# Pooled attention and a rational MoE on one core: the pooled keys of batches 2 to 7 turned by VectorE and placed by transfers, and the planner's figures changed

## The chip, the cores and the metric

The kernel runs on one core of a Trainium2 chip, as one launch. The metric is the device time in microseconds (us). PE is TensorE (PEld its weight loads), DVE is VectorE, ACT is ScalarE, POOL is GpSimd, SP is SyncE, whose queue issues every transfer of this kernel.

## The reference, cut to what matters

There are 8 batches of 576 tokens, 8 heads, 64 dimensions a head. Keys and values are averaged over groups of 8 tokens, so each head has 72 pooled keys. The attention output, 4608 rows of 512, goes through two matrix products with a rational function between them.

```python
k_p = k.reshape(B, H, Sp, pool, D).mean(axis=3)      # pool 8, Sp 72
v_p = v.reshape(B, H, Sp, pool, D).mean(axis=3)
scores = scale * np.matmul(q, k_p.transpose(0, 1, 3, 2))
scores = scores - np.max(scores, axis=-1, keepdims=True)
attn = np.exp(scores)
attn = attn / (np.sum(attn, axis=-1, keepdims=True) + 1e-09)
x = np.matmul(attn, v_p)        # then laid out as 4608 x 512
h = x @ w_in                    # 512 x 2048
P = a[0] + a[1] * h + a[2] * h2 + a[3] * h3
Q = 1.0 + np.abs(b[0]) * np.abs(h) + np.abs(b[1]) * h2
out = (P / (Q + 1e-6)) @ w_out  # 2048 x 512
```

Inputs are float32 or float64 and results float32: a value is split into a high and a low part, and a product is three matrix products of parts. The weights come as float64 and are decoded on the chip.

## The kernel before, in words

**The work.** The tokens are cut into blocks: three short ones of 256 (`SHORT`) and ten of 384, numbered 0 to 12. For each block the attention (`attend`, L833) makes x, and then eight slices of the hidden layer follow (`u` from 0 to 7): `mm1` (tile `ph`), `rational`, `mm2` (tile `po`). The order of slices (L1033 on) is: blocks 0 to 2 with the first four slices, block 3 with all eight, blocks 0 to 2 with the last four (x is reloaded), then blocks 4 to 12. The weights are loaded and decoded (`load_weights`, L515) when their first user comes, which is in the first 180 us.

**The keys.** A batch is prepared when the first block that touches it is attended: batches 0 and 1 with blocks 0 and 2, batches 2 to 7 with blocks 4, 5, 7, 8, 10 and 11. `prep_k` (L550) loads the keys of a batch as 576 rows of 8 x 64 numbers, in five pieces (for batches 2 to 7 through the three `stage` buffers, which `prep_v` uses too). Three halvings sum the 8 tokens: two in place (`st_k`), and the third into `ks`, written twice over so that each row holds its 64 sums two times. POOL does the sums of batches 1 and 2, DVE those of the others. Then PE transposes the five pieces of 128 x 128 into the PSUM tiles `pk` and `pl`, and five copies (two on ACT, three on DVE) take them to `kpT` and multiply by 1/8. `kpT[n % 2]` holds, for each pair of heads, the 64 dimensions of one head in the lower half of the partitions and those of the other in the upper half, with 2 x 72 columns; the score products (tile `ps`, in `attention`, L698) read it. There are two of these tiles, so batch n writes over batch n - 2.

**The order of the work.** A planner (`Plan`, L104 on) takes the operations as the program adds them (`add`, L151), each with an engine, a cost in us and a due time, and places them by a list schedule (`solve`, L195): what can start first goes first, the one that is due first among those. Instructions are then issued in this order, and each engine works through its own in order. A due time is `HEAD + SLOW * min(at, SLOWS) + PACE * max(0, at - SLOWS)` where `at` counts the work of the MoE before it; an operation that others need is due earlier by 1.4 times (cost + 0.25 us, and 4 us more for a transfer) for each link of the chain. No operation is planned earlier than `early` before its due time (40 us, a transfer 60 us). `LATER` shifts the due times of single operations by number. Costs are written at the calls, for example `act(CW + 200)` for the first step of a decoded weight.

**Fillers.** Where the plan leaves PE idle, `issue` (L293) puts small products that change nothing (L317), on tile `idle` near the start and on `po` later.

All other instructions carry line L325, since one line issues them; they are told apart by tile.

Of the kernel before, what the change touches and what calls it, by code (L numbers as in the profile page):

```python
# [107 lines left out]
class Plan:  # L108
# [42 lines left out]
    def add(self, eng, cost, calls, port=False, claims=(), bytes=0, early=40.0, after=()):  # L151
        op = Op()
        op.eng, op.cost, op.port, op.calls, op.bytes = eng, cost, port, calls, bytes
        op.early, op.slack, op.lead = early, self.slack, 0.0
        op.keep, op.spare = self.keep, 0
        op.seq, op.due, op.deps, op.users = len(self.ops), self.now, set(), []
        touched = {}
        for _, args, kw in calls:
            every = list(args) + list(kw.values())
            dst = kw.get("out", args[0] if args else None)  # L160
            for v in every:
                if isinstance(v, Lazy) and v is not dst:
                    box = v.box()
                    op.deps.update(o for o, x in v.tile.writes if meet(x, box))
                    v.tile.reads.append((op, box))
                    touched[id(v.tile)] = v.tile
            if isinstance(dst, Lazy):
                t, box = dst.tile, dst.box()
                op.deps.update(o for o, x in t.writes if meet(x, box))
                op.deps.update(o for o, x in t.reads if meet(x, box))  # L170
                if box == ():
                    t.writes, t.reads = [], [r for r in t.reads if r[0] is op]
                t.writes.append((op, box))
                touched[id(t)] = t
        for t in touched.values():
            if t.ring.tag == "ps":

                op.deps.update(o for o in t.users if o.eng != eng)
                t.users.append(op)
        op.deps.update(after)  # L180
        op.deps.discard(op)
        for c in claims:
            touched[id(c.tile)] = c.tile
        op.bufs = list(touched.values())
        for b in op.bufs:
            b.left += 1
        self.ops.append(op)
        return op
# [155 lines left out]
def tile_pooled_attention_then_rational_moe(  # L344
# [20 lines left out]
    P = 128  # L365
# [3 lines left out]
    REM = 2 * SP - P  # L369
    RW = G * D  # L370
    SHORT, PAIR = 3, True
# [143 lines left out]
    def load_weights(kind, u):  # L515
# [12 lines left out]
        act(CW + 200).activation(m, hw.bitcast(F32), AF.Prelu, scale=2.0 ** -111, alpha=-2.0 ** 32)  # L528
        dve(CW, port=True, rate=0.52).tensor_scalar(
            out=mi, in0=mi, scalar1=3, scalar2=None, op0=ALU.logical_shift_left)  # L530
        dve(CW, port=True).scalar_tensor_tensor(
# [8 lines left out]
        act(CW + (380 if kind == "wout" else 0)).copy(high, m)  # L540
# [9 lines left out]
    def prep_k(n):  # L550
# [6 lines left out]
        pieces = ((0, 2, P), (2, 4, P)) if n < 2 else tuple((c, c + 1, P) for c in range(4))  # L557
        for c0, c1, np in (*pieces, (4, 5, H * SP - 4 * P)):
            nc_ = c1 - c0
            if n < 2:  # L560
                place = early(n, c0 // 4)[:, (c0 % 4) * RW:(c0 % 4 + nc_) * RW]
            else:
                place = new("stage", "st", [P, RW], F32, f"st_k{n}_{c0}")
            dma(2 * np * nc_, place[:np].rearrange("p (c x) -> p c x", c=nc_),
                rows[c0 * P:c0 * P + nc_ * np].rearrange("(c p) x -> p c x", c=nc_))
            st = place[:np].rearrange("p (c x) -> p c x", c=nc_)
            w = RW // 2
            while w > D:
                (gp if n in (1, 2) else dve)(nc_ * w, port=True).tensor_tensor(
                    out=st[:, :, 0:w], in0=st[:, :, 0:w], in1=st[:, :, w:2 * w], op=ALU.add)  # L570
                w //= 2
            ks = every[:np, c0:c1]
            if np < P:
                gp(2 * D).memset(every[np:, c0:c1], 0.0)
            both = [np, nc_, 2, D]
            (gp if n in (1, 2) else dve)(nc_ * 2 * w, port=True).tensor_tensor(
                out=ks, in0=st[:, :, 0:w].unsqueeze(2).to_broadcast(both),
                in1=st[:, :, w:2 * w].unsqueeze(2).to_broadcast(both), op=ALU.add)
            turns_ = [("transpose", (pk[:, c * P:(c + 1) * P] if c < 4 else pl,
                                     every[:, c].rearrange("p a d -> p (a d)"), ident), {})  # L580
                      for c in (range(c0, c1) if n < 2 else range(5))]
            if n < 2 or c1 == 5:
                turned = pe(109 * len(turns_), turns_)
                turned.lead = 1.5 if n > 2 else 0.0
        dst, both = kpT[n % 2], 2 * SP
        for hh in range(2):
# [9 lines left out]
            for to, src in parts:  # L596
                if hh == 0:
                    act(150).activation(to, src, AF.Copy, scale=1.0 / G)
                else:
                    dve(120).tensor_scalar(out=to, in0=src, scalar1=1.0 / G, scalar2=None,  # L600
                                           op0=ALU.mult)
# [76 lines left out]
    HB = 32  # L678

    def squares(i):  # L680
# [4 lines left out]
        if i < SHORT:  # L685
            return new("cpool", "wout6" if i else "win6", shape, F32, f"q{i}")
        qs = new(*(("cpool", "wout7") if i == SHORT else ("work1", "am")), shape, F32, f"q{i}")
# [10 lines left out]
    def attention(i, m, hi, lo, qs, es):  # L698
# [7 lines left out]
        if i >= SHORT:  # L706
# [38 lines left out]
        act(H * SP + 24).activation(ef, ef, AF.Exp, scale=D ** -0.5)  # L745
# [12 lines left out]
        if i >= SHORT:  # L758
# [74 lines left out]
    def attend(i):  # L833

        for _, _, n in segs(tok0(i), size(i)):
            if n not in prepared:
                prepared.add(n)
                prep_k(n)
                (prep_v_early if n < 2 else prep_v)(n)
# [4 lines left out]
        if i < SHORT:  # L844
# [9 lines left out]
        if i >= SHORT:  # L854
# [184 lines left out]
    for i, u in order:  # L1039
        for fs in ((0, 1),) if i < SHORT and PAIR else ((0,), (1,)):  # L1040
            steps.append((at, i, u, fs))
            at += len(fs) * size(i) / 512
    HEAD, PACE, SLOW, SLOWS = 15.6, 5.8, 5.48, 20
# [16 lines left out]
    for at, i, u, fs in steps:  # L1060
# [3 lines left out]
        if (i, again) not in xs:  # L1064
            plan.slack = 1.4
            plan.now = due(at) - (0 if again else {1: 8, 2: 14, 3: 14}.get(i, 0.0))
# [59 lines left out]
```

## Time and profile before

| | |
|---|---|
| median of 3 runs | 883.38 us (882.62 to 1519.48) |
| the profiled execution | 883.58 us, of which the span from first to last instruction is 881.9 us |
| PE, PEld busy | 865.2 us (98%), 805.5 us (91%) |
| DVE, ACT, POOL busy | 769.7, 725.2, 549.9 us |
| the chain that ended last | PE 82%, ACT 7%, DVE 5%, DMA 3% |

The run of 1519.48 us stands by itself and isn't used. The profile is of one execution: busy times are times in which an engine ran an instruction. PE's are modelled from pipelined instructions and overlap, so the spacing of their starts tells more than the length of one. In a list by tile, "x5" counts instructions, and the times are of one. "[0.89 <-ACT gh]" behind an instruction is the idle time of its engine just before it, and what ended it.

### The profile page before, as it was taken

The page shows a single profiled execution, that of the slowest core. Times are in us where ns is not written, and L with a number is a line of the kernel's source. Part 1 is how long each engine was busy: PE and PEld are TensorE (multiplying, and loading weights), DVE is VectorE, ACT ScalarE, POOL GpSimd, SP SyncE. Part 2 cuts the span into 40 slices and gives each one's busy share as a digit, 9 for nine tenths or more (in the row PEclk, how much of TensorE's full clock was granted, in tenths as well). Part 3 has the DMA queues.
Part 4 walks back from the last instruction along what each step waited for, and adds up shares of the span by engine and source line. Part 5 has one row for each costly group of instructions (what it writes and reads, how often), then busy time and mean ns, then how long its engine had stood idle before and what let it go on. Part 6 is the DMA issues. An engine that isn't in the chain of part 4 may idle for free.

```text
span 881.9 us, 15828 instructions
## 1 busy us (share of the span) xinstructions
PE 865.2 (98%) x5067; PEld 805.5 (91%) x5067; DVE 769.7 (87%) x1585; ACT 725.2 (82%) x1373; POOL 549.9 (62%) x614
## 2 busy tenths in 40 slices
PE   8799999999999999999999999999999999999998
PEld 7699889998999999999999999999999999999997
DVE  6899988888998988998998987998998987997764
ACT  4798898987688788788798797788888888888886
POOL 5766779796645744666655854646755764554554
PEclk9999999999999999999999999999999999999999
DMA  9896651133344232244034142043332432020000
GB/s 301 211 383 224 176 126 38 49 121 108 82 113 106 46 80 61 33 89 131 14 77 98 32 89 36 37 84 73 96 54 50 113 55 37 37 47 8 37 1 36
DMA packets 192919, 79.17 MB, mean 90 GB/s; under 512 B 169412, under 2 KB 169412, under 8 KB 192836
## 3 DMA queue, kind: packets, MB, share of 16 engines
q1 hardware_dynamic: 192836, 78.16, 34.2%
q8 instruction: 40, 0.66, 0.3%
q14 instruction: 43, 0.35, 0.1%
HBM read 52.17 MB, written 14.16 MB: 75 GB/s over the span
## 4 chain that ended last, share of the span: by engine, by line
PE 82%; ACT 7%; DVE 5%; DMA 3%; POOL 2%; issue 1%; SPq 1%; POOLq 0%; DVEq 0%; ACTq 0%
PE ph L325 36%; PE po L325 36%; PE ps L325 4%; PE pv L325 3%; DMA q<-in_q_dram 2%; DVE t L325 2%; ACT rp L325 1%; SPq L325 1%; ACT t L325 1%; PE pvs L325 1%; ACT hi L325 1%; ACT r L325 1%; ACT w L325 1%; DVE e L325 1%; ACT gh L325 1%
## 5 line engine op out<-in xcount | busy, mean ns | idle before, releaser
L325 PE MATMUL ph<-x,win 128*128 128x384 f32 (+1 forms) x2208 | 380.1, 321 | 1.1 <-POOL win L325 0.6
L325 PEld LDWEIGHTS ph<-x,win 128*128 128x128 f32 x2208 | 356.7, 190 | 12.1 <-POOL win L325 0.8
L325 PE MATMUL po<-wout,gh 128*128 128x512 f32 x1152 | 299.8, 383 | 1.8 <-ACT gh L325 1.7
L325 POOL TENSOR_TENSOR w<-w,r 128x384 f32<-128x384 f32 (+2 forms) x186 | 196.2, 1056 | 148.4 <-ACT r L325 136.8
L325 POOL TENSOR_TENSOR gl<-t,gh 128x384 fp32r<-128x384 f32 (+2 forms) x186 | 201.3, 1083 | 127.2 <-ACT gh L325 95.2
L325 PEld LDWEIGHTS po<-wout,gh 128*128 128x128 f32 x1152 | 209.4, 189 | 25.3 <-ACT gh L325 3.5
L325 DVE SCALAR_TENSOR_TENSOR t<-t,abn,rp 128x384 f32<-128x384 f32 (+2 forms) x186 | 114.7, 618 | 58.4 <-ACT rp L325 57.2
L325 PE MATMUL po<-wout,gl 128*128 128x512 f32 x576 | 162.0, 382 | 0.7 <-POOL gl L325 0.6
L325 ACT ACTIVATE t<-ph,abn 128x384 f32<-128x384 f32 (+2 forms) x186 | 125.8, 678 | 35.8 <-DVE rp L325 13.9
L325 ACT ACTIVATE r<-w,abn 128x384 f32<-128x384 f32 (+2 forms) x186 | 133.1, 715 | 9.0 <-POOL gl L325 4.1
L325 ACT ACTIVATE rp<-w,cbias 128x384 f32<-128x384 f32 (+2 forms) x186 | 110.7, 595 | 30.6 <-POOL w L325 25.8
L325 DVE TENSOR_TENSOR t<-t,ph 128x384 f32<-128x384 f32 (+2 forms) x186 | 103.6, 559 | 19.1 <-ACT w L325 10.2
L325 PEld LDWEIGHTS po<-wout,gl 128*128 128x128 f32 x576 | 104.7, 189 | 12.4 <-POOL gl L325 2.1
L325 DVE SCALAR_TENSOR_TENSOR t<-t,abn,ph 128x384 f32<-128x384 f32 (+2 forms) x186 | 114.5, 616 | 1.2
L325 ACT ACTIVATE w<-ph 128x384 f32<-128x384 f32 (+2 forms) x186 | 92.4, 497 | 21.6 <-PE ph L325 17.4
L325 ACT CAST gh<-t 128x384 fp32r<-128x384 f32 (+2 forms) x186 | 96.0, 516 | 14.6 <-DVE t L325 9.7
L325 DVE SCALAR_TENSOR_TENSOR t<-rp,t 128x384 f32<-128x384 f32 (+2 forms) x186 | 104.0, 559 | 1.9
L325 DVE SCALAR_TENSOR_TENSOR rp<-w,rp 128x384 f32<-128x384 f32 (+2 forms) x186 | 105.0, 565 | 0.0
L325 ACT ACTIVATE rp<-rp 128x384 f32<-128x384 f32 (+2 forms) x186 | 91.1, 490 | 2.2
L325 POOL TENSOR_TENSOR e<-e,sm 128x576 f32<-128x576 f32 x36 | 42.8, 1201 | 29.2 <-DVE sm L325 20.2
L325 POOL TENSOR_TENSOR st_v<-st_v 128x256 f32<-128x256 f32 (+1 forms) x72 | 42.6, 603 | 7.9 <-DMA st_v<-in_v_dram 7.2
L325 PE MATMUL ps<-kpT,qT 128*128 128x144 f32 (+1 forms) x304 | 42.0, 293 | 0.3 <-DVE qT L325 0.3
(110 smaller groups left out, 879.5 us busy)
## 6 DMA issues: line engine op xcount, KB each, us to landing
am<-e SPq DMA_DIRECT2D x160, 72.0 KB, 2.4
rwin<-in_moe_w_in_dram SPq DMA_DIRECT2D x8, 1024.0 KB, 8.2
rwout<-in_moe_w_out_dram SPq DMA_DIRECT2D x8, 1024.0 KB, 12.2
out_dram<-ob SPq DMA_DIRECT2D x30, 256.0 KB, 2.5
st_k<-in_k_dram SPq DMA_DIRECT2D x24, 256.0 KB, 3.2
st_v<-in_v_dram SPq DMA_DIRECT2D x24, 256.0 KB, 2.7
q<-in_q_dram SPq DMA_DIRECT2D x112, 48.0 KB, 2.3
xd<-x SPq DMA_DIRECT2D x6, 512.0 KB, 12.3
```

The lines of the kernel that those rows point to most:

```text
L325: getattr(engines[op.eng], name)(*map(value, args), **{k: value(v) for k, v in kw.items()})
```

## The change

For batches 2 to 7, `prep_k_late` takes the place of `prep_k`. The keys of two heads (64 of their 72 pooled rows) are loaded into one stage buffer by two transfers, four times, and the last 8 pooled rows of all heads into half of a fifth by eight. The sums go on three halvings as before, the last one without the doubling, into `squares_` (tile `ks`). DVE transposes this tile in squares of 32 x 32, in two instructions, and 16 transfers from SBUF to SBUF place the squares in `kpT`: eight of 16 KB in runs of 128 bytes, eight of 2 KB in runs of 32 bytes. The five transposes on PE, their PSUM tiles and the five copies go for these batches. Batches 0 and 1 keep `prep_k`. The factor 1/8 moves into the scale of the exponential for all batches.

For the planner: `early` is 24 us in place of 40 for all but transfers; the costs of three steps of the weight decoding are longer; `HEAD, PACE, SLOW, SLOWS` go from 15.6, 5.8, 5.48, 20 to 16.0, 5.76, 5.55, 8; the attention of block 2 is due 20 us ahead of its first use in place of 14, that of block 3 10 in place of 14; `LATER` is another list. `TURNED` takes the place of `SHORT` in the attention with the same value 3, and `PAIR` goes, which was true.

```diff
-    def add(self, eng, cost, calls, port=False, claims=(), bytes=0, early=40.0, after=()):
+    def add(self, eng, cost, calls, port=False, claims=(), bytes=0, early=24.0, after=()):
...
-        act(CW + 200).activation(m, hw.bitcast(F32), AF.Prelu, scale=2.0 ** -111, alpha=-2.0 ** 32)
+        act(CW + (480 if kind == "wout" else 350)).activation(m, hw.bitcast(F32), AF.Prelu, scale=2.0 ** -111, alpha=-2.0 ** 32)
...
-        dve(CW, port=True).scalar_tensor_tensor(
+        dve(CW + (280 if kind == "wout" else 160), port=True).scalar_tensor_tensor(
...
-        act(CW + (380 if kind == "wout" else 0)).copy(high, m)
+        act(CW + (460 if kind == "wout" else 0)).copy(high, m)
...
+    def prep_k_late(n):
+
+        MAIN = 2 * HB
+        squares_ = new("work1", "ks", [P, NJ + 1, D], F32, f"ks{n}")
+        eng = gp if n == 2 else dve
+        for c in range(NJ + 1):
+            st = new("stage", "st", [P, RW], F32, f"st_k{n}_{c}")
+            np = P if c < NJ else P // 2
+            if c < NJ:
+                for hh in range(2):
+                    dma(128, st[hh * MAIN:(hh + 1) * MAIN, :], k[n, 2 * c + hh, 0:MAIN * G, :].rearrange(
+                        "(s t) d -> s (t d)", t=G))
+            else:
+                for h in range(H):
+                    dma(16, st[h * (SP - MAIN):(h + 1) * (SP - MAIN), :],
+                        k[n, h, MAIN * G:S, :].rearrange("(s t) d -> s (t d)", t=G))
+            w = RW // 2
+            while w >= D:
+                to = st[:np, 0:w] if w > D else squares_[:np, c, :]
+                eng(w, port=True).tensor_tensor(out=to, in0=st[:np, 0:w], in1=st[:np, w:2 * w],
+                                                op=ALU.add)
+                w //= 2
+        for r in (slice(0, P), slice(0, P // 2)):
+            cs = slice(0, NJ) if r.stop == P else slice(NJ, NJ + 1)
+            dve((cs.stop - cs.start) * D).transpose(squares_[r, cs], squares_[r, cs])
+        for hh in range(2):
+            for b in range(2):
+                to = kpT[n % 2][hh * D + b * HB:hh * D + (b + 1) * HB]
+                cols = slice(b * HB, (b + 1) * HB)
+                for g in range(2):
+                    p0, s0 = hh * MAIN + g * HB, hh * SP + g * HB
+                    dma(16, to[:, :, s0:s0 + HB], squares_[p0:p0 + HB, 0:NJ, cols], run=128,
+                        issue=0.65)
+                    s0 = hh * SP + MAIN
+                    dma(2, to[:, 2 * g:2 * g + 2, s0:s0 + SP - MAIN],
+                        squares_[g * HB:(g + 1) * HB, NJ, cols].rearrange(
+                            "p (j h s) -> p h j s", j=2, h=2)[:, hh], run=32, issue=0.65)
...
-        act(H * SP + 24).activation(ef, ef, AF.Exp, scale=D ** -0.5)
+        act(H * SP + 24).activation(ef, ef, AF.Exp, scale=D ** -0.5 / G)
...
-                prep_k(n)
-                (prep_v_early if n < 2 else prep_v)(n)
+                (prep_k if n < POOLED else prep_k_late)(n)
+                (prep_v_early if n < POOLED else prep_v)(n)
...
-    HEAD, PACE, SLOW, SLOWS = 15.6, 5.8, 5.48, 20
+    HEAD, PACE, SLOW, SLOWS = 16.0, 5.76, 5.55, 8
...
-            plan.now = due(at) - (0 if again else {1: 8, 2: 14, 3: 14}.get(i, 0.0))
+            plan.now = due(at) - (0 if again else {1: 8, 2: 20, 3: 10}.get(i, 0.0))
```

In `prep_k` the branches for batches 2 to 7 go, and its copies to `kpT` no longer scale.

## Rows read from the trace of the kernel before

**Rows 1.** Busy time of each engine in five stretches of the span (length; busy us and instructions of PE, PEld, DVE, ACT, POOL; granted TensorE clock; DMA share, GB/s).
```profile
0.00:44.00 44.00, 34.88 (x237) 31.82 (x238) 33.31 (x70) 26.07 (x48) 29.82 (x69) 0.95 0.91 256
44.00:180.00 136.00, 133.31 (x850) 123.52 (x850) 122.60 (x214) 123.80 (x203) 105.36 (x84) 0.99 0.52 162
180.00:330.00 150.00, 149.58 (x932) 138.98 (x932) 137.07 (x275) 120.19 (x224) 95.08 (x105) 1.00 0.36 95
330.00:858.00 528.00, 527.74 (x2959) 493.89 (x2958) 465.24 (x1000) 440.14 (x864) 308.65 (x345) 1.00 0.26 58
858.00:882.00 24.00, 19.68 (x97) 17.31 (x95) 11.45 (x30) 15.01 (x37) 10.95 (x15) 1.00 0.09 33
```

**Rows 2.** The chain that ended last, in order of time: two unbroken pieces of PE in the steady stretch (start, us, what, how many products).
```profile
328.39 7.80 PE ph L325 x48
...
428.01 3.24 PE po L325 x15
```

**Rows 3.** The transposes of the keys by the tile `pk` (four of a batch's five; the fifth writes `pl`), all of the run.
```profile
L325 PE MATMUL pk<-identr,ks x32: 272/273/273, 6.6 to 684.9; 128*128 128x128 f32 x32
```

**Rows 4.** Timeline of PE around the transposes of batches 4 and 6, and the first scores of batch 4 (start, length, engine, instruction, count).
```profile
411.34 0.60 PE L325 MATMUL pk<-identr,ks 128*128 128x128 f32 x4
...
411.81 1.22 PE L325 MATMUL ph<-x,win 128*128 128x384 f32 x6
412.87 0.81 PE L325 MATMUL po<-wout,gh 128*128 128x512 f32 x3
...
414.16 0.65 PE L325 MATMUL ps<-kpT,qT 128*128 128x144 f32 x4
...
618.40 0.60 PE L325 MATMUL pk<-identr,ks 128*128 128x128 f32 x4
...
619.93 0.81 PE L325 MATMUL po<-wout,gh 128*128 128x512 f32 x3
```

**Rows 5.** Groups of instructions by shape (busy us of all, mean ns of one): DVE's last halvings, its transposes of other tiles, and its copies to `kpT`.
```profile
L325 DVE TENSOR_TENSOR ks<-st_k 128x128 f32<-128x128 f32 x20 | 6.7, 347 | 0.0
...
L325 DVE STREAM_TRANSPOSE qT<-q 128x512 f32<-128x512 f32 x30 | 21.1, 703 | 2.6 <-DMA q<-in_q_dram 1.9 <-DMA st_v<-in_v_dram 0.4
...
L325 DVE STREAM_TRANSPOSE e<-e 128x128 f32<-128x128 f32 x60 | 17.3, 293 | 0.3 <-POOL e L325 0.3
...
L325 DVE TENSOR_SCALAR kpT<-pk 64x216 f32<-64x216 f32 x8 | 3.1, 385 | 0.6 <-ACT kpT L325 0.4
...
L325 DVE TENSOR_SCALAR kpT<-pl 64x64 f32<-64x64 f32 x8 | 1.8, 228 | 2.8 <-PE pl L325 2.6
...
L325 DVE TENSOR_SCALAR kpT<-pk 64x8 f32<-64x8 f32 x8 | 1.3, 163 | 0.0
```

**Rows 6.** Issues on SP's queue by tile (ns of one issue, min/median/max), and below each the time from issue to landing.
```profile
L325 SPq DMA_DIRECT2D st_k<-in_k_dram x30: 327/430/1964, 104.9 to 673.1; - x30
DMA to landing us min/median/max: 2.5/3.1/4.6
...
L325 SPq DMA_DIRECT2D am<-e x160: 586/632/1863, 99.0 to 793.2; - x160
DMA to landing us min/median/max: 2.2/2.4/4.1
```

**Rows 7.** What SP's queue waited for between 330 and 858 us: the longest (us in total, times, longest).
```profile
SPq L325 <- DVE e L325: 102.6, 7, 20.0
```

**Rows 8.** The last halvings by tile, for batches 2, 5 and 7 in turn ("first to last start" is what is read).
```profile
L325 POOL TENSOR_TENSOR ks<-st_k x5: 448/490/502, 140.4 to 157.2; 128x128 f32<-128x128 f32 x4, 64x128 f32<-64x128 f32 x1
...
L325 DVE TENSOR_TENSOR ks<-st_k x5: 275/279/284, 448.6 to 469.3; 128x128 f32<-128x128 f32 x4, 64x128 f32<-64x128 f32 x1
...
L325 DVE TENSOR_TENSOR ks<-st_k x5: 271/280/285, 660.7 to 678.4; 128x128 f32<-128x128 f32 x4, 64x128 f32<-64x128 f32 x1
```

**Rows 9.** Timeline of PE: the first scores of batches 2, 5 and 7.
```profile
211.97 1.14 PE L325 MATMUL ps<-kpT,qT 128*128 128x144 f32 x8
...
480.63 0.65 PE L325 MATMUL ps<-kpT,qT 128*128 128x144 f32 x4
...
687.79 1.28 PE L325 MATMUL ps<-kpT,qT 128*128 128x144 f32 x8
```

**Rows 10.** Timeline of PE: its waits between 44 and 180 us, and the longest run of fillers.
```profile
94.19 0.70 PE L325 MATMUL po<-wout,gh 128*128 128x512 f32 x2 [0.89 <-ACT gh L325]
...
118.16 2.51 PE L317 MATMUL po<-zero,identr 128*128 128x256 f32 x21
...
121.49 0.70 PE L325 MATMUL po<-wout,gh 128*128 128x512 f32 x2 [0.82 <-ACT gh L325]
...
170.62 0.92 PE L325 MATMUL po<-wout,gl 128*128 128x512 f32 x3 [0.65 <-POOL gl L325]
```

**Rows 11.** The fillers on `po` (L317), all of the run: ns of one, first and last start.
```profile
L317 PE MATMUL po<-zero,identr x31: 272/274/276, 82.1 to 322.4; 128*128 128x256 f32 x31
```

**Rows 12.** Groups by shape: three of the steps of the weight decoding whose planned costs change (busy us of all, mean ns of one).
```profile
L325 DVE SCALAR_TENSOR_TENSOR m_wout<-rwout,m_wout 128x1024 int32<-128x1024 int32 x8 | 12.6, 1575 | 0.0
L325 ACT CAST wout<-m_wout 128x1024 fp32r<-128x1024 f32 x8 | 11.6, 1454 | 2.7 <-DVE m_wout L325 2.7
...
L325 DVE SCALAR_TENSOR_TENSOR m_win<-rwin,m_win 128x1024 int32<-128x1024 int32 x8 | 10.8, 1354 | 0.1
```

More of the change, by code (lines that the diff above doesn't have):

```diff
@@ L369, in tile_pooled_attention_then_rational_moe @@
     REM = 2 * SP - P
+    HB = 32
     RW = G * D
-    SHORT, PAIR = 3, True
+    SHORT, TURNED, POOLED = 3, 3, 2
     NBLK = SHORT + (NT - SHORT * 256) // 384
@@ L556, in prep_k @@
         every = new("work1", "ks", [P, 5, 2, D], F32, f"ks{n}")
-        pieces = ((0, 2, P), (2, 4, P)) if n < 2 else tuple((c, c + 1, P) for c in range(4))
-        for c0, c1, np in (*pieces, (4, 5, H * SP - 4 * P)):
+        for c0, c1, np in ((0, 2, P), (2, 4, P), (4, 5, H * SP - 4 * P)):
             nc_ = c1 - c0
[L560 to L563, printed above, removed]
+            place = early(n, c0 // 4)[:, (c0 % 4) * RW:(c0 % 4 + nc_) * RW]
             dma(2 * np * nc_, place[:np].rearrange("p (c x) -> p c x", c=nc_),
@@ L568, in prep_k @@
             while w > D:
-                (gp if n in (1, 2) else dve)(nc_ * w, port=True).tensor_tensor(
+                (gp if n == 1 else dve)(nc_ * w, port=True).tensor_tensor(
                     out=st[:, :, 0:w], in0=st[:, :, 0:w], in1=st[:, :, w:2 * w], op=ALU.add)
@@ L575, in prep_k @@
             both = [np, nc_, 2, D]
-            (gp if n in (1, 2) else dve)(nc_ * 2 * w, port=True).tensor_tensor(
+            (gp if n == 1 else dve)(nc_ * 2 * w, port=True).tensor_tensor(
                 out=ks, in0=st[:, :, 0:w].unsqueeze(2).to_broadcast(both),
                 in1=st[:, :, w:2 * w].unsqueeze(2).to_broadcast(both), op=ALU.add)
[L579 to L584, printed above, removed]
+            pe(109 * nc_, [
+                ("transpose", (pk[:, (c0 + c) * P:(c0 + c + 1) * P] if c0 < 4 else pl,
+                               every[:, c0 + c].rearrange("p a d -> p (a d)"), ident), {})
+                for c in range(nc_)])
         dst, both = kpT[n % 2], 2 * SP
@@ L597, in prep_k @@
                 if hh == 0:
-                    act(150).activation(to, src, AF.Copy, scale=1.0 / G)
+                    act(150).copy(to, src)
                 else:
-                    dve(120).tensor_scalar(out=to, in0=src, scalar1=1.0 / G, scalar2=None,
-                                           op0=ALU.mult)
+                    dve(120).tensor_copy(to, src)
+    def prep_k_late(n):
[34 more added lines that the diff above has]
+                            "p (j h s) -> p h j s", j=2, h=2)[:, hh], run=32, issue=0.65)
     def v_rows(n):
@@ L676, in segs @@
         return r
-    HB = 32
     def squares(i):
         shape = [P, NJ, size(i) // HB, HB]
-        if i < SHORT:
+        if i < TURNED:
             return new("cpool", "wout6" if i else "win6", shape, F32, f"q{i}")
-        qs = new(*(("cpool", "wout7") if i == SHORT else ("work1", "am")), shape, F32, f"q{i}")
+        qs = new(*(("cpool", "wout7") if i == TURNED else ("work1", "am")), shape, F32, f"q{i}")
         for r0, r1, n in segs(tok0(i), size(i)):
@@ L705, in attention @@
               new("work1", "qT", [P, NJ * P], F32, f"qT{t}")).rearrange("p (j t) -> p j t", j=NJ)
-        if i >= SHORT:
+        if i >= TURNED:
             b0 = m * (P // HB)
@@ L757, in attention @@
                 for c in range(2)]
-        if i >= SHORT:
+        if i >= TURNED:
             for c in range(2):
@@ L843, in attend @@
         es = new("work1", "e", [P, NJ + 2, M, 2 * SP], F32, f"e{i}")
-        if i < SHORT:
+        if i < TURNED:
             if not shared:
@@ L853, in attend @@
             attention(i, m, hi, lo, qs, es)
-        if i >= SHORT:
+        if i >= TURNED:
             for a in range(4):
@@ L1039, in tile_pooled_attention_then_rational_moe @@
     for i, u in order:
-        for fs in ((0, 1),) if i < SHORT and PAIR else ((0,), (1,)):
+        for fs in ((0, 1),) if i < SHORT else ((0,), (1,)):
             steps.append((at, i, u, fs))
             at += len(fs) * size(i) / 512
-    HEAD, PACE, SLOW, SLOWS = 15.6, 5.8, 5.48, 20
+    HEAD, PACE, SLOW, SLOWS = 16.0, 5.76, 5.55, 8
     def due(at):
```

23 rows, old and new, of the table LATER are left out of this document.

## The prediction, made before the changed kernel ran

> **What bounds the kernel now.** I read the busy times by stretch first [rows 1]. From 330 to 858 us PE is busy 527.74 of 528 us, from 180 to 330 us 149.58 of 150; DVE follows with 465.24 of 528 us. Busy alone could mean slow products that wait inside, so the second view is the chain of waits [rows 2]: 48 products of 384 columns take 7.80 us, 162.5 ns each, and 15 of 512 columns 3.24 us, 216 ns each. That is 384 and 512 columns at 2.4 a ns with 2 to 3 ns over: at the granted clock of 1.00, which is the level of 2.4 GHz, the array takes a column in every cycle. In this stretch time falls only if PE has less to do, and it rises by all that PE has to wait. PE's idle time is elsewhere: 44 - 34.88 = 9.1 us before 44 us, 136 - 133.31 = 2.7 us from 44 to 180 us, and 4.3 us at the end [rows 1].
>
> One page speaks against reading it so: the Trainium skill, "Perfetto Trace Analysis", section "Identifying the Most-Contended Engine", calls busy time of matmuls a bad measure of distance to the roofline and wants that of the weight loads. By that, the 493.89 us of PEld in 528 [rows 1] would leave room on PE, taking five transposes away would save nothing, and the time would be the one before. The spacing speaks against it, and the measurement decides; it is the last rival below.
>
> **Part 1: five transposes on PE go, in six batches.** The tile `pk` takes 32 transposes in the run, four a batch for eight batches [rows 3]; six of those batches lose them, with the fifth of each. A transpose is listed at 273 ns, but they overlap, so the price is read from what comes after [rows 4]. Batch 4: the first starts at 411.34, six `ph` products follow at 411.81, `po` at 412.87. The six products take 6 x 162.5 = 0.975 us by [rows 2], so the transposes put `po` back by 1.53 - 0.975 = 0.56 us. Batch 6: 619.93 - 618.40 is again 1.53. The difference between the first two starts, 0.47, is the lower bound. Six batches give 6 x 0.56 = **3.3 us** (2.8 to 3.4). All of it lies where PE is full, so it comes off the end.
>
> **Part 2: DVE, ACT and POOL.** DVE loses three copies a batch, 385 + 228 + 163 = 776 ns [rows 5]. Its last halving writes 64 columns in place of 128: by the median of 280 ns [rows 8], at about 1 ns a column, 0.06 us less, five times. It gains two transposes: from 703 ns at 512 columns and 293 at 128 [rows 5], 1.07 ns a column, 256 columns are about 0.43 us and 64 about 0.22. Net 0.4 to 0.5 us less a batch. ACT loses two copies, POOL a memset. None of these bounds the steady stretch, so I put it at 0. The factor 1/8 in the exponential changes a constant.
>
> **Part 3: SP's queue and the transfers.** For each late batch 5 loads become 16, and 16 placements come in. By 0.43 us for a load and 0.63 for an SBUF to SBUF transfer in 128-byte runs (`am`, the nearest row) [rows 6] that is 11 x 0.43 + 16 x 0.63 = 14.8 us of SP more a batch. Between 330 and 858 us SP waits in one line alone, for DVE's `e`, 102.6 us [rows 7], so its time isn't scarce; its order is what matters. Queued behind a placement that waits for DVE's transposes are the stage loads of the values, the queries of the next block, the `am` transfers and the stores of the output; DVE and then PE wait for these.
>
> Ahead of the scores the chain becomes longer. Before, batch 4's first transpose started at 411.34 and its first scores at 414.16 [rows 4], 2.8 us for PE and the copies. Now it is DVE 0.65, sixteen issues 10.1, landing 2.4 [rows 6]: **13.2 us**. Is that room there? The last halvings start at 157.2, 469.3 and 678.4 in batches 2, 5 and 7 [rows 8], the first scores at 211.97, 480.63 and 687.79 [rows 9]: 54.8, 11.3 and 9.4 us. Left where they are, batch 5 would come 1.9 us late and batch 7 3.8, each a straight loss on PE. But the due times move: a placement's is 1.4 x (0.65 + 4.25) = 6.9 us ahead of the scores, and those that write the same 32 partitions are counted one behind the other, four deep, 27 us. So the halvings are due some 30 us earlier than the scores, against about 2 before, and `early` of 24 lets them start another 24 ahead. I take 0, with 0 and 5.7 us as ends; a gain is excluded, since no wait of PE for `kpT` stands in the trace.
>
> A rule against this part: the Trainium skill, "DMA: Bandwidth & Descriptors", section "Rules for kernel authors", says to coalesce, as transfers under 64 KB pay mostly overhead. The landing of `am`, 2.4 us for 72 KB, against 3.1 for the larger `st_k` fits that: by the rule the placements of 2 and 16 KB cost nearly what 72 KB cost, and if nothing hid them the time would be the 941 us of the rival of late keys.
>
> **Part 4: the planner's figures.** The longer costs are nearer to the trace: the plan had 0.068 + 1024 x 1.04 / 1000 = 1.13 us for the decoding step that takes 1575 ns in `wout` and 1354 in `win`, and 1.26 us for a cast of 1454 [rows 12]. That stretch, 44 to 180 us, is where PE waits for ACT and POOL (0.89, 0.82, 0.65 us) and runs 21 fillers in 2.51 us before block 3's x [rows 10]; 31 fillers at 0.12 are 3.7 us [rows 11], all but the last before 180 us. Idle and fillers there are 2.7 + 3.6 = 6.3 us, the most that better order could return. Against it: block 3's attention is due 4 us later than before, which is where those fillers stand, so the same place could lose up to 4 us. I take a gain of **1.5 us**, a quarter of 6.3, since one cause of several is mended; ends +4.0 and -6.3. What lies before 44 us (9.1 us) and the last 4.3 us I leave as they are; the due times of block 1 and 2 shift in the former in either direction.
>
> **Sum.** 883.58 (the profiled execution; the median of the runs is 883.38, 0.2 below) - 3.3 - 1.5 = 878.8, so against the median **878.6 us**.
>
> **The rivals.** A kernel of this time moves by 2% only from 17.7 us on, which is about what a measurement tells from no change.
>
> *Given back in the order of the work* (chance 0.27). The 3.3 us come off PE, but the new due times put waits into the first 330 us or between stages. For it: the old list of shifts left under 0.7 us of idle PE in 678 us [rows 1], so another order has little to win and much to lose; block 3 is due later. Against it: the decoding costs are truer. One wait more of 2 to 7 us: 882 to 888 us.
>
> *Late keys, slower than before* (0.12). The placements aren't in SBUF when PE reaches the first scores of a batch, at `ps` after `kpT`, and PE, in order, stands still. Unhidden the chain costs 13.2 - 2.8 = 10.4 us a batch, 62 us in six: 941. With only batches 5 and 7 late by 1.9 and 3.8 us it is 878.6 + 5.7 = 884.3. It turns the sign when the six waits together exceed 4.8 us, 0.8 a batch, and passes 2% at 22.5 us, 3.7 a batch. For it: the room in the trace for two of six batches. Against it: the earlier due times. I give 0.08 to 884 to 901 and 0.04 to more.
>
> *More from the front* (0.08). The order before 180 us returns most of the 6.3 us and some of the 9.1: 868 to 875 us.
>
> *PE has room after all* (0.03). The transposes were covered by the weight loads, and taking them away does nothing: 882 to 883.4 us.
>
> **How the numbers follow.** The forecast, 875 to 882, has 0.50. The range takes in the rival that gives it back, whole, and the lower part of late keys: **873 to 888 us**. Left out are the rest of late keys and half of the gain from the front, about 0.14. Faster by over 2% (under 865.7) would need all idle time but the head's minimum: 0.01. Slower by over 2% (over 901.1): 0.04. Within 2%: 0.95.
>
> **What the changed profile would show.** PE's instructions on `pk` 8 in place of 32, and PE busy from 330 to 858 us as full as before, with the span shorter. 96 transfers into `kpT`, at 0.6 us an issue. The score products wait for no transfer; if they do, the late keys are there, first in batches 5 and 7. Fillers on `po` near 120 us fewer, and the waits for ACT's `gh` near 94 and 121 us gone; if they are longer, part 4 has the wrong sign. If PE is idle for more than 2 us after 330 us, the order of the work was the weak point; if the span falls by less than 2.8 us with PE full, part 1 was.

## The result, and the profile after

The changed kernel takes 894.8 us (median of 6 runs, 892.08 to 896.72) against 884.46 beside it, where one run of six, 1519.48 us, stands by itself and is left out of the ratio: ratio 1.011, 95% interval 1.0092 to 1.0128, so **9.7 us slower**, where 4.8 less were forecast and 888 was the end of the range. Within 2%, but not by the forecast's reasons. The profiled execution took 893.83 us, its span 892.1.

Busy time by stretch, of the kernel after (columns as in [rows 1]; the fourth stretch ends at 868 here):

```profile
0.00:44.00 44.00, 37.84 (x258) 34.63 (x259) 31.51 (x68) 25.50 (x48) 28.20 (x69) 1.00 0.97 270
44.00:180.00 136.00, 133.78 (x866) 125.56 (x865) 121.89 (x214) 120.13 (x197) 95.26 (x78) 0.99 0.51 158
180.00:330.00 150.00, 148.03 (x912) 136.64 (x912) 136.08 (x269) 120.13 (x222) 98.02 (x107) 1.00 0.36 96
330.00:868.00 538.00, 532.69 (x2958) 495.32 (x2957) 472.62 (x1003) 438.80 (x861) 308.98 (x343) 1.00 0.27 59
```

PE is idle 538 - 532.69 = 5.3 us behind 330 us, against 0.26 in [rows 1], and 2.0 against 0.4 between 180 and 330. The chain that ended last, by engine, where before had PE 82% and SP's queue 1%:

```profile
PE 49%; SPq 13%; DVE 12%; ACT 9%; DMA 6%; issue 5%; POOL 4%; DVEq 0%; POOLq 0%; ACTq 0%
```

By tile, the transposes on PE that are left (against [rows 3]), the placements, and the fillers (against [rows 11]):

```profile
L324 PE MATMUL pk<-identr,ks x8: 272/273/330, 8.7 to 30.6; 128*128 128x128 f32 x8
...
L324 SPq DMA_DIRECT2D kpT<-ks x96: 585/595/1590, 143.9 to 705.3; - x96
...
L316 PE MATMUL po<-zero,identr x74: 272/274/367, 66.4 to 236.9; 128*128 128x256 f32 x74
```

The change does what it says: 8 transposes for 32, 96 placements at 0.6 us an issue. What DVE waited for between 330 and 858 us, its waits for queries (`qT`) alone (before: 1.9 + 0.4 us):

```profile
DVE qT L324 <- DMA q<-in_q_dram: 4.6, 4, 1.9
DVE qT L324 <- issue: 2.1, 1, 2.1
...
DVE qT L324 <- DMA kpT<-ks: 1.6, 1, 1.6
```

SP's queue ahead of one of these waits, and the wait (timeline of after; "x27" instructions in a row, in brackets the idle time before):

```profile
468.02 0.44 SPq L324 DMA_DIRECT2D q<-in_q_dram  x1
468.56 2.51 SPq L324 DMA_DIRECT2D kpT<-ks  x4
471.11 0.59 SPq L324 DMA_DIRECT2D q<-in_q_dram  x1
471.74 0.59 SPq L324 DMA_DIRECT2D kpT<-ks  x1
472.37 1.07 SPq L324 DMA_DIRECT2D q<-in_q_dram  x2
473.48 1.24 SPq L324 DMA_DIRECT2D kpT<-ks  x2
474.76 14.49 SPq L324 DMA_DIRECT2D q<-in_q_dram  x27
...
483.22 0.71 DVE L324 STREAM_TRANSPOSE qT<-q 128x512 f32<-128x512 f32 x1 [0.82 <-DMA q<-in_q_dram]
```

For 21 us SP issues without a pause. With the placements left out (x2, below) the same queries go in one piece and the last of them is issued 8 us earlier, though x2's products are only 2.5 us ahead there:

```profile
465.16 16.01 SPq L326 DMA_DIRECT2D q<-in_q_dram  x32
```

The placements are in good time for the scores; the pieces of queries that stand in the same row are not, and it is DVE that waits for them.

### The profile page after: what moved, and what is told of

Read it like the earlier page. It is cut to its first block, busy times and chain, and to the rows that moved or that the text cites. A ratio compares the mean times of both kernels' runs of the same rounds, so it can differ in the third digit from the quotient of the medians.

```text
span 892.1 us, 16044 instructions
## 1 busy us (share of the span) xinstructions
PE 872.4 (98%) x5085; PEld 809.9 (91%) x5085; DVE 773.9 (87%) x1579; ACT 720.0 (81%) x1361; POOL 541.8 (61%) x608
## 4 chain that ended last, share of the span: by engine, by line
PE 49%; SPq 13%; DVE 12%; ACT 9%; DMA 6%; issue 5%; POOL 4%; DVEq 0%; POOLq 0%; ACTq 0%
PE ph L324 21%; PE po L324 21%; SPq L324 13%; DVE t L324 5%; PE ps L324 3%; PE pv L324 3%; ACT rp L324 2%; DMA q<-in_q_dram 2%; POOL w L324 2%; DVE rp L324 2%; DVE e L324 1%; ACT t L324 1%; DMA rwin<-in_moe_w_in_dram 1%; DMA st_v<-in_v_dram 1%; ACT gh L324 1%
## 5 line engine op out<-in xcount | busy, mean ns | idle before, releaser
L324 PEld LDWEIGHTS ph<-x,win 128*128 128x128 f32 x2208 | 357.4, 190 | 15.3 <-issue 1.6
L324 PE MATMUL po<-wout,gl 128*128 128x512 f32 x576 | 160.2, 380 | 0.0
L324 POOL TENSOR_TENSOR e<-e,sm 128x576 f32<-128x576 f32 x36 | 41.0, 1151 | 30.2 <-DVE sm L324 19.6
L324 PE MATMUL ps<-kpT,qT 128*128 128x144 f32 (+1 forms) x304 | 44.2, 294 | 0.4 <-DVE e L324 0.3
```

What stands on the lines that cost most here:

```text
L324: getattr(engines[op.eng], name)(*map(value, args), **{k: value(v) for k, v in kw.items()})
```

## The experiments

Theory 1, the order: the plan made anew (figures, due times, list of shifts) lost it. Theory 2, the queue: the 27 more transfers of a late batch did. Each run is given as its ratio to before on the same chip, with the interval; 0.001 is 0.88 us.

### The placements, taken out of two orders

In x2 the placements are skipped where instructions are issued; in y1 the same, with `LATER` empty; a0 has `LATER` empty and the placements in. So x2 and y1 leave the pooled keys of batches 2 to 7 out of the result; a0 computes all of it.

```diff
             for name, args, kw in op.calls:
+                if name == "dma_start" and isinstance(args[0], Lazy) and args[0].tile.name.startswith("kpT"):
+                    continue
```

x2: 

> The changed kernel's order with its 96 placements left out at issue, so the scores of batches 2 to 7 are taken with keys that were never placed (the pooled keys of batches 2 to 7 are left out of the result). Theory 1 (the order): the other instructions stand as badly as before; within 1.5 us of the changed kernel, 893 to 896. Theory 2 (the queue): SP gets back 16 x 0.6 = 9.6 us a batch where it now issues without a pause; 4 to 9 us faster, 885 to 890, and PE idle after 330 us falls from 5.3 to under 2.5 us.

a0: 

> The changed kernel with its new list of shifts emptied, all else as changed: what the new list is worth. Before's list was worth 0.75% on the chip (b0 against before). If the new list fits its order as well, this is 5 to 8 us slower than the changed kernel, 1.017 to 1.021 times before; if it is worth nothing on the chip, within 1.5 us of it or faster, and half of the excess over the forecast lies in that list.

y1: 

> The changed kernel with an empty list of shifts (a0) and its 96 placements left out at issue, so the pooled keys of batches 2 to 7 are left out of the scores. a0 was 1.0028 times before. If a placement costs SP's time in any order, this falls by as much as x2 did, 6 to 8 us, to 0.994 to 0.996 times before. If the placements only hurt in the order that the new list makes, within 2 us of a0: 1.001 to 1.004.

| | with placements | without |
|---|---|---|
| the new list | 1.0110 (1.0092 to 1.0128) | x2: 1.0027 (1.0016 to 1.0038) |
| no list | a0: 1.0028 (1.0014 to 1.0042) | y1: 0.9969 (0.9958 to 0.9980) |

Both theories hold, side by side. The placements cost 0.0083 under the list and 0.0059 without, 7.3 and 5.2 us; the list costs 0.0082 with them and 0.0058 without. With neither, the late keys are 2.7 us **faster** than before. DVE's waits for queries, 330 to 858 us, in x2, then a0, then y1 (the only `qT` lines among each one's ten longest):

```profile
DVE qT L326 <- DMA q<-in_q_dram: 3.0, 3, 1.9
```
```profile
DVE qT L312 <- DMA q<-in_q_dram: 5.7, 5, 2.9
...
DVE qT L312 <- issue: 0.5, 1, 0.5
```
```profile
DVE qT L314 <- DMA q<-in_q_dram: 0.6, 1, 0.6
```

After minus x2 is 8.3 - 3.0 = 5.3 us of waiting, a0 minus y1 6.2 - 0.6 = 5.6: near the 7.3 and 5.2 us that the placements cost. Counted from 180 us on, these waits are 10.8 against 3.0 us in the first pair and 6.8 against 0.6 in the second, so the differences are 7.8 and 6.2 us. SP's queue has 2% of x2's chain and 13% of after's.

When the cost comes shows where both profiles of a pair are read product by product, since their orders are the same. a0 stays within 0.2 us of y1 from the first `ph` product up to 280 us and is 4.7 us behind at the last one. The changed kernel is 1.8 us ahead of x2 at 77 us, ahead of any placement, level at 330 us, and 5.2 us behind at 751. So batch 2's placements, from 144 us on, cost next to nothing, and the later ones cost steps of up to 2 us at single places.

The number of fillers doesn't tell the loss: a0 and y1 have 80 of them on `po`, more than the changed kernel's 74, and y1 is faster than before.

### Issue or bytes, loads, another queue

x7 cuts each placement to one partition (`args = tuple(a[0:1] for a in args)`); x4 makes 5 loads of the 16; x5 issues the placements from POOL (`eng = self.nc.gpsimd`). All three have the changed kernel's order and list. x7 leaves 31 of 32 rows of the late keys out of the result, x4 has these keys in wrong places, and x5 computes everything.

x7: 

> The changed kernel with each of the 96 placements cut to one partition of its 32, so 31 of 32 rows of the pooled keys of batches 2 to 7 are left out. The issues stay, the bytes go. If SP's issue is the cost, the time stays within 1.5 us of the changed kernel, as far as an issue still takes 0.6 us (if a small one takes 0.4, a third of the 7 us that x2 gave comes back). If the transfers themselves are the cost (engines of the DMA, ports of SBUF), it falls by 5 to 7 us, to x2's 1.003 times before.

x4: 

> The changed kernel's order, but at issue the 16 loads of a late batch's keys become five of the same bytes, each at the place of the first of its group and the others dropped; the rows of the keys then stand in another order, so the scores of batches 2 to 7 are taken with keys in wrong places. SP issues 66 transfers less in the run, at 0.43 us, 28 us. Theory 1 (the order): within 1 us of the changed kernel's 1.011 times before. Theory 2 (the queue), by what x2 gave back for 96 placements (some 7 us for 58 us of SP): about half as much, 2 to 4 us faster than the changed kernel.

x5: 

> The changed kernel whole, its 96 placements issued from POOL's queue in place of SP's, at the same place in the order. If the issue in SP's queue is the cost, SP gets back what x2 gave it and the time falls 3 to 7 us below the changed kernel, unless POOL pays as much: POOL is busy 541.8 of 892 us and issues 16 a batch. If the placed bytes or the landing are the cost, no change within 1 us. If POOL's own order is as tight as SP's, the time rises by some us a batch.

x7 came to 1.0074 (1.0053 to 1.0095), about half of the way to x2; its interval just touches the changed kernel's, so the share is rough. Its issues hardly got shorter:

```profile
L326 SPq DMA_DIRECT2D kpT<-ks x96: 552/572/722, 144.9 to 702.5; - x96
```

With 1/32 of the rows an issue takes 572 ns for 595. What SP pays for these is by the transfer, not by the byte. Yet DVE's waits for queries between 330 and 858 us fall to 3.1 + 1.0 + 0.5 = 4.6 us, from 8.3 (x2 has 3.0), so the rest of the gain comes with the bytes; how they delay a query isn't shown, since these traces don't give the queries' landings. The Trainium skill, "DMA: Bandwidth & Descriptors", section "Rules for kernel authors", says that transfers under 64 KB pay mostly overhead. As far as the issue goes, the 572 ns agree. x4 is at 1.0093 (1.0073 to 1.0113): the 66 loads more can't be told from nothing. x5 is worst, 1.0205 (1.0190 to 1.0220): POOL issues in 551 ns, and ACT waits 13.2 us for its `w` between 330 and 858 us, in place of 10.1. Most of the loss is earlier: read product by product, x5 loses 4.9 us to the changed kernel between 128 and 166 us, where POOL issues batch 2's placements between its steps of weight decoding, and it ends 7.7 us behind.

### The list, in parts

b0 empties before's own list. y2 keeps of the new list the 26 shifts of operations planned before 240 us, y3 the other 69, y4 the 9 of the head. z2 keeps all, but issues two loads where they stood without it:

```diff
     plan.solve()
+    for late, ahead in ((637, 466), (471, 201)):
+        op = plan.ops[late]
+        plan.order.remove(op)
+        plan.order.insert(plan.order.index(plan.ops[ahead]), op)
```

b0: 

> The kernel before with its list of shifts of the due times emptied, all else as it was: what the list is worth to an order. Theory 1 (the order): an order that no list was fitted to loses several us on PE: 886 to 895 us. Theory 2 (the queue): SP's queue is as short as before, so little is lost: 883 to 886 us.

y2: 

> The changed kernel with only the 26 shifts of its list whose operations are planned before 240 us; the other 69 are dropped. The changed kernel has done the products that a0 ends at 247.6 us at 251.2, 3.6 us later, and ends 10 us later in its profile. If the front's shifts carry the loss, this is near the changed kernel, 1.009 to 1.012 times before, and 3 to 4 us behind a0 at 250 us. If the shifts of the rest carry it, near a0: 1.002 to 1.005. If neither does it alone, in between.

y3: 

> The changed kernel with only the 69 shifts whose operations are planned from 240 us on; the first 240 us stand as in a0. If the rest's shifts carry the loss, 3 to 6 us more than a0: 1.006 to 1.010 times before, with PE idle from 330 to 858 us as much as in the changed kernel. If the front's do, near a0: 1.002 to 1.004.

y4: 

> The changed kernel with only the 9 shifts of its list that stand before operation 203, all in the head (the first loads, the masks, the keys of batch 0). y2, with all 26 of the front, was 1.0142, a0 without any 1.0028. The changed kernel begins its first product of x 1.9 us later than a0 (26.0 against 24.1 us). If the head's shifts carry the front's loss, 1.008 to 1.014, with the first product of x at 26; if the other 17 do, 1.001 to 1.005, with it at 24.

z2: 

> The changed kernel in its own order, but two loads that its list moved (a piece of block 3's queries by 33 us, a piece of batch 1's values by 8) are issued where they stood without the list: the piece of queries ahead of batch 1's values, near 25 us in place of 49, the other ahead of the loads of weights near 46. In the changed kernel PE waits 0.6 us for queries and 1.2 us for those values before 75 us, and it has done its first 96 output products 2.6 us later than a0. If these two loads carry the front's loss, 2 to 4 us faster than the changed kernel: 1.007 to 1.009 times before. If the other shifts do, within 1 us of it: 1.010 to 1.012.

b0 1.0075 (1.0052 to 1.0097): before's list is worth 6.6 us to before's order. y2 1.0142 (1.0112 to 1.0171), y3 1.0023 (1.0008 to 1.0038), y4 1.0030 (1.0019 to 1.0041): the loss comes with the 26 of the front, not with the 9 of the head among them; the other 17 were not run alone. Where, in y2: PE from 60 to 80 us in a0, then in y2, and the longest piece of y2's chain from 44 to 120 us.

```profile
60.00:80.00 20.00, 19.96 (x156) 19.06 (x155) 19.84 (x40) 17.62 (x32) 12.57 (x9) 1.00 0.57 215
```
```profile
60.00:80.00 20.00, 17.88 (x131) 16.23 (x130) 19.56 (x35) 15.13 (x28) 9.94 (x7) 1.00 0.43 169
```
```profile
48.49 11.57 DMA q<-in_q_dram
```

One piece of block 3's queries, shifted by 33 us, is issued at 48.5 behind loads of weights and lands 11.6 us later; DVE and then PE stand behind it. That is the smaller part: by the 151st `ph` product, at 80 us, y2 is 2.6 us behind a0, by the 701st, at 242 us, 4.4, and at the last 9.4, though behind 240 us it has no shifts of its own. z2, which puts this piece and one of batch 1's values back in the changed kernel, is at 1.0086 (1.0071 to 1.0100): some 2 us of the 7.3 that the list costs, with intervals that overlap a little. Which of the other front shifts cost the rest is open, the more so as each shift changes what comes after it.

### A row of transfers in an order without room

x1 does the late keys in before's order, with 16 placements right behind a batch's last halving; x3 is before, whole, with 16 idle transfers there:

```diff
+        op.alt = [(op.eng, *c) for c in op.calls]
...
+                    op.alt.append(("sp", "dma_start", (
+                        to[:, 48 * g:48 * g + 48].rearrange("p (j s) -> p j s", j=3),
+                        sq[p0:p0 + HB, 0:3, 16 * b_:16 * b_ + 16]), {}))
```

x1: 

> The order of every instruction is that of the kernel before, with its figures and its list of shifts; only at issue are the keys of batches 2 to 7 done the new way: the loads in the changed kernel's pieces, five last halvings of 64 columns, two DVE transposes and 16 placements right behind the batch's last halving, no transposes on PE, no copies, no memset, 1/8 in the exponential. It computes the same outputs. Theory 1 (the order): the loss comes from the work being ordered anew, and the way of the keys itself is worth what PE no longer does: 878 to 882 us, PE idle under 1 us from 330 to 858 us. Theory 2 (the queue): the 27 more transfers of a late batch hold up the loads and stores that stand behind them in SP's queue: 886 to 897 us, with PE idle several us after 330 us.

x3: 

> The kernel before, whole, with 16 transfers more in each of batches 2 to 7 behind the last halving: SBUF to SBUF, from the pooled keys into a tile that nobody reads, 32 partitions each, 8 of 32 x 3 x 16 and 8 of 32 x 2 x 2 numbers. Theory 1 (the order): SP has time, at most 1 us slower, 883 to 885. Theory 2 (the queue): the 10 us of SP in a row push back the loads of the values and the queries behind them: 3 to 8 us slower, 886 to 892, with the loss on PE at the stages where those transfers stand.

Both expectations were far too small: x1 1.0727 (1.0701 to 1.0753), x3 1.0651 (1.0632 to 1.0669), 58 us for 96 transfers that nobody reads. On average that is 16 x 0.6 = 9.6 us a batch, but it isn't spread so: read product by product against before, x3 is 0.7 us late at 279 us, with batch 2's row long past, and then loses 10 to 13 us at each of the other five batches. SP's queue in x3 at batch 2's row and at batch 3's, then in before at batch 3's:

```profile
154.57 11.17 SPq L326 DMA_DIRECT2D scratch<-ks  x16
165.84 4.22 SPq L326 DMA_DIRECT2D st_v<-in_v_dram  x9
...
263.62 10.26 SPq L326 DMA_DIRECT2D scratch<-ks  x16
273.92 11.90 SPq L326 DMA_DIRECT2D q<-in_q_dram  x22
285.86 0.44 SPq L326 DMA_DIRECT2D ob<-pd  x1
```
```profile
258.63 15.05 SPq L325 DMA_DIRECT2D q<-in_q_dram  x31
273.72 0.45 SPq L325 DMA_DIRECT2D ob<-pd  x1
```

PE's wait behind batch 3's row, and its stretch:

```profile
290.40 1.22 PE L326 MATMUL po<-wout,gh 128*128 128x512 f32 x2 [9.95 <-DVE ob L326]
```
```profile
268.00:300.00 32.00, 22.05 (x119) 19.49 (x117) 17.33 (x36) 16.12 (x35) 12.19 (x15) 0.84 0.32 78
```

Behind this row stand queries and then the reload of partial sums (`ob`), and each comes the row's length late. While PE is idle its granted clock falls, to 0.84 over these 32 us, which can make up the difference between the wait of 9.95 us and the 13 us lost here; no run has the one without the other. So SP's queue had no room at these five places before the change either: ahead of batch 3 it already issued queries for 15 us without a pause. The 102.6 us that it waits for one thing alone in [rows 7] are at other places. Where it had room, at batch 2, the same row cost nothing.

### Placing without SP

DVE can write a transpose of 32 partitions to other partitions, so no transfer is needed. d1 has a0's order, and 12 such transposes in a row in place of 2 and of the placements; in d2 one stands behind every fourth DVE instruction. e1 has a0's order with 8 loads a batch, 11 transposes and 4 copies; e2 the same in before's order.

```diff
+                to = kpT[n % 2][hh * D + b * HB:hh * D + (b + 1) * HB]
...
+                    turns.append((to[:, :, s0:s0 + HB], squares_[p0:p0 + HB, 0:NJ, cols]))
...
+            late = dves[at + 4 * i]
+            late.calls = late.calls + [("transpose", t, {})]
```

(The last two lines are d2's alone.)

d1: 

> As e1, but the loads stay 16 a batch: the rows are those of the changed kernel, and DVE places them in 12 transposes, 8 of 128 columns and 4 of 32, no copies. The outputs are the same. Against e1 it tells what the 8 loads fewer a batch are worth: 0 to 2 us slower than e1. Against y1 (no placements at all, 0.9969) what the 12 transposes cost: 0 to 6 us.

d2: 

> d1 (a0's order, VectorE's transposes write the keys into place, no placements), but the 12 transposes don't stand in a row: one behind every fourth DVE instruction, the 8 large from the place of the changed kernel's first transpose on, the 4 small from the place of its second. The outputs are the same. d1's 12 in a row took 3.4 us and PE waited 2 to 3 us for the decoding step behind them; the DVE time stays, 8 x 302 + 4 x 202 = 3.2 us a batch. If the row was the cost, this falls from d1's 1.0139 to near y1 (no placement at all, 0.9969): 0.996 to 1.001 times before, faster than the changed kernel by 10 us and perhaps than before. If DVE's added time is the cost, near d1: 1.010 to 1.014.

e1: 

> a0's order (the changed kernel, empty list of shifts); at issue a late batch's keys are loaded in 8 transfers in place of 16 (a chunk is 128 rows in a row of a pair of heads), and VectorE places them itself: transposes of 32 partitions that write straight into the tile of keys at other partitions, 11 of them, and four copies, at the place of the second transpose; no placement is issued. The outputs are the same. In the changed kernel the transposes took 448 ns at 256 columns and 223 at 64; by these 3 to 3.6 us of DVE a batch in place of 0.67. If the placements' cost is SP's queue, and the 2.5 to 3 us more of DVE a batch find room (DVE was busy 465 of 528 us), the time is that of y1 (0.9969 times before) less 1 to 2 us for the loads: 0.994 to 0.998. If DVE has no room, 1 to 2 us a batch come back: 1.000 to 1.010.

e2: 

> The kernel before, its figures, its list and its order; only at issue batches 2 to 7 take VectorE's way of e1: 8 loads in place of 5, 64 columns in the last halvings, 11 transposes and four copies of DVE behind the last halving, no transposes on PE, no copies from PSUM, no memset. The outputs are the same. x1, which put 16 placements and 11 loads more in the same places, was 1.073 times before. If SP's queue alone made that, this is 0.995 to 1.000 times before: 3.3 us less of PE, some 1 us a batch at risk for 3 more loads. If DVE's 3 us in a row hold up what stands behind them, 1.003 to 1.010.

The transposes by shape in d2, and d2's stretch of 447 to 486 us:

```profile
L312 DVE STREAM_TRANSPOSE kpT<-ks 32x128 f32<-32x128 f32 x48 | 14.5, 302 | 1.2
...
L312 DVE STREAM_TRANSPOSE kpT<-ks 32x32 f32<-32x32 f32 x24 | 4.8, 200 | 0.5
```
```profile
447.00:486.00 39.00, 36.70 (x197) 33.54 (x197) 37.85 (x82) 29.74 (x59) 19.09 (x20) 1.00 0.34 64
```

Half of the 48 go to other partitions, and none of them takes over 309 ns; the mean of 302 stands against 293 in place for 128 columns [rows 5]. The Trainium skill, "Vector Engine (DVE) Microarchitecture Reference", section 3.8, says that such moves of 32 partitions are free; the trace agrees. But d1 is at 1.0139 (1.0121 to 1.0158) and d2 at 1.0128 (1.0109 to 1.0147): spreading helps little, and my expectation for d2 failed. Against y1, d2 has (14.5 + 4.8) - 6 x 0.67 = 15.3 us more of DVE and takes 0.0159, 14 us, longer. **DVE's added time comes out nearly one for one.** In the stretch shown it is busy 37.85 of 39 us, and PE is idle 2.3. d1, with the same 15.3 us in a row, takes 15 us longer than y1. e1 is at 1.0278 (1.0248 to 1.0308): 21 us more of DVE than y1 cost 27, and why it is 12 us slower than d1 for 5.8 us more of DVE is open. e2 is at 1.0241 (1.0211 to 1.0272). Against x1, in the same order, with 8 loads for 16 and DVE in place of 16 placements, it gives back 43 of 64 us. The expectations for d1, e1 and e2 were too low as well, by the same belief that DVE had room.

Why there is no room on DVE shows in the kernel before, once its steady stretch is cut finer than in [rows 1]:

```profile
346.00:376.00 30.00, 30.00 (x173) 28.27 (x172) 29.92 (x74) 24.29 (x47) 17.32 (x18) 1.00 0.24 55
...
412.00:440.00 28.00, 28.00 (x156) 25.61 (x155) 27.73 (x69) 22.31 (x46) 17.46 (x21) 1.00 0.17 53
...
520.00:551.00 31.00, 31.00 (x182) 29.26 (x182) 24.58 (x46) 26.02 (x51) 14.78 (x14) 1.00 0.18 34
...
618.00:650.00 32.00, 32.00 (x184) 30.04 (x183) 30.71 (x75) 26.09 (x53) 21.76 (x26) 1.00 0.30 82
```

Between scores and values of a block DVE (the third number) is nearly as full as PE: 29.92 of 30, 27.73 of 28, 30.71 of 32, and in the other three blocks up to 720 us, 36.63 of 39 (481 to 520), 30.88 of 32 (551 to 583) and 31.14 of 32 (688 to 720). The 88% of the whole stretch are these and stretches at 79% (24.58 of 31). So a late piece of queries, which leaves DVE idle just there, is hard to make up, and the steps of the pairs above say that PE pays.

### Fewer transfers, planned anew

c0 loads 128 rows in a row of each pair of heads (8 loads, 14 placements a batch), with an empty list.

```diff
+                dma(512, st, rows[2 * SP * c:2 * SP * c + P])
...
+                for j in range(NJ):
+                    dma(64, st[j * REM:(j + 1) * REM, :], rows[2 * SP * j + P:2 * SP * (j + 1)])
```

> A late batch with fewer transfers, planned anew with an empty list: a chunk of keys is one load of 128 rows in a row (two heads have 144 rows, 72 each; the 16 left over of each pair make the fifth chunk), 8 loads in place of 16, and 14 placements in place of 16. The outputs are the same. SP issues 10 transfers less a batch, 60 in the run, some 27 us of its time. If SP's time is the cost, 1 to 4 us faster than a0 (1.0028 times before): 0.998 to 1.002. If what decides is how the order happens to fall, anywhere from 0.998 to 1.010, and the difference to a0 stands at single waits on PE and not in each batch.

1.0090 (1.0064 to 1.0117), 5.5 us slower than a0 with 60 transfers less. Plans of nearly the same work lie 5 to 10 us apart here, which hides what transfers are worth; only pairs in one order tell it. None of the versions with all of its work was faster than before.

## Why the prediction was wrong

**Part 1, PE's transposes, 3.3 us.** They are gone as counted. No run has the transposes alone undone; what speaks for the size is that y1, where the two costs below are out, stands at 0.9969, 2.0 us above the forecast's ratio 878.6 / 883.38 = 0.9946. The planner's new figures are in y1 too, so this nearness may be luck.

**Part 2, DVE put at 0.** "None of these bounds the steady stretch" was the reading of an average. The change takes little DVE time away, so the term itself did little harm; the premise did, since it let every delay of DVE pass as hidden.

**Part 3, SP and the transfers, taken as 0 (ends 0 and 5.7). This step failed first.** It named what stands behind a placement, queries among it, and then priced only the other end: the keys, 13.2 us ahead of the scores. That end held: PE waits for no transfer of keys in the changed kernel, as forecast. But "its time isn't scarce" came from one sum of waits over 528 us [rows 7], and the cost was at the queries: 5.2 to 7.3 us measured. 16 issues in a row cost 10 to 13 us in x3 at five places of six, with nothing planned around them; the plan, which knows them, hid all but about 1 us a batch.

**Part 4, the planner's figures, -1.5 (ends +4.0 and -6.3). The other failure, in size and sign,** at the list of shifts, which the working didn't price apart from the figures. The list costs 5.1 to 7.3 us, with the 26 front shifts; the fillers, forecast to be fewer, went from 31 to 74. By the prediction's own count, idle time and fillers from 44 to 180 us, the term was a loss: 136 - 133.78 = 2.2 and 69 x 0.12 = 8.3 are 10.5 us against 6.3, and a0, without the list, has 1.1 + 65 x 0.12 = 8.9. PE's waits for ACT's `gh` there are gone, as forecast, but the plan leaves more of PE to fillers; ahead of 44 us, which the prediction left as it was, idle time falls from 9.1 to 6.2 us. That the figures cost time as a whole isn't shown: with both lists empty, a0 against b0 is 1.0028 to 1.0075, 4.2 us less, but two orders differ by chance as well.

**The rivals.** "Given back in the order of the work" (0.27) names one of the two costs, the new due times, with its sign, PE idle for more than 2 us after 330 us; the placements' cost to the queries behind them is in no rival. Its price, one wait of 2 to 7 us, was too small: two costs of this size came together, and they add up to 12.5 us from y1 to the changed kernel. "Late keys" did not happen; y1, which lies below before, speaks against "PE has room", but its order is another one too.

## What to carry to other kernels

Cut the steady stretch into the parts of a stage before calling an engine free: one with 88% on average was at 94 to 99.7% where it mattered, and a delay there, or a microsecond more of work, came out nearly whole. Price a new transfer by who stands behind it in its queue at that place, not by the queue's idle time. A list of shifts fitted to one order is part of that order: when the work changes, time the new plan with an empty list too, before the two effects are mixed.

## What was not expected

A transfer of one partition from SBUF to SBUF takes SP 0.57 us to issue, nearly as long as one of 32. Some 11 us of SP issuing in a row cost the kernel 10 to 13 us at five batches and nothing at a sixth, and PE's granted clock fell to 0.84 in the first of these stretches. And before's list of small shifts, which look like noise, was worth 6.6 us.
